# Expert steps and half of a feed-forward layer put in a hand-given order, with weight conversions cut into three parts

## The chip, the core and the metric

The kernel runs on one core of a Trainium2 chip. The core has a matrix engine (PE, TensorE; PEld is its weight load), a vector engine (DVE), a scalar engine (ACT), GpSimd (POOL) and a queue engine (SP) that issues most of the transfers. Each engine works through its own list of instructions in order and waits at an instruction until what it needs is there. The metric is the device time of one execution in microseconds.

## The reference

Three layers follow one another. Linear attention gives x, 2304 tokens by 512. A mixture of 8 experts sends each token to the expert of its largest gate value; an expert is a 512 x 1024 matrix, a ReLU and a 1024 x 512 matrix, and the result is scaled by the gate. The second layer is dense:

```
h = np.maximum(np.einsum('ecd,edf->ecf', disp, w1), 0.0)
y = np.einsum('ecf,efd->ecd', h, w2)
...
h = x @ w_in
g = np.where(h > 0.0, h, alpha * (np.exp(np.minimum(h, 0.0)) - 1.0))
return (g @ w_out).astype(np.float32)
```

w_in (512 x 2048) and w_out (2048 x 512) come in 64-bit floating point; all else is 32-bit.

## The kernel before, in words

Every float32 matrix is split in a high and a low word (names ending in h and l), and a product is three matmuls: high by high, high by low, low by high (`three`, L588 to L590; L877 to L879 in the last product). The high word is a copy on ACT (L480), the low word a subtraction (L483) on the engine that the caller names.

The attention part sorts the tokens by expert, writes rows to a table in DRAM and leaves in `ids` which row goes where. Then come 64 **expert steps**, eight for each of the experts 0 to 7 (r); u numbers them from 0 to 63 and fc is u's place within its expert. An expert works on a window of columns of the sorted tokens, WIN = 352, 336, 320, 304, 288, 288, 272 and 256 wide. Step u (`step`) loads the weights of step u + 3, does h(u) (12 matmuls into `ph`; then hh on ACT, L607, and hl on DVE, L608), then y(u - 1) (12 matmuls into four `acc`), and splits the weights of step u + 2. In y the third matmul of each triple needs hl.

During expert 0 the 18 tiles of sorted tokens are brought in: a gather on POOL's queue (L494, three buffers, so the gather of tile a + 3 waits for the turn of tile a), a scaling on DVE (L500), and a turn of four transposes on PE (L507) with a copy on ACT (L508) into xT. QUOTA says how many tiles a step turns, and in step 6 (fc == 6) what is left is turned and the next expert's window xh, xl is cut out of xT in one piece (L582, L583). After step 36 a branch (L729) skips a part for overfull experts.

The **second layer** works in four quarters of its hidden units (NQ; four weight units in each) over six blocks of 384 tokens: 96 steps of 12 matmuls into `ph` (`ffn_h`) and 9 into `acc` (`ffn_out`, two steps later), with e on ACT, g on DVE, gh on ACT and gl on DVE between. The first time a block is split into yh (ACT) and yl (POOL) and stored; in later quarters it is loaded.

The 64-bit weights of the second layer are **converted** by integer arithmetic, in 32 halves (w_in and w_out of 16 units): `magnitude` on ACT (L655), five DVE operations in `convert` (L663 to L667), then `split`, with the low word on POOL. `cvt_a` and `cvt_b` have one buffer each. The first quarter's eight halves are converted during the expert steps from u = 28 on, one every third step.

What sets the order: the attention part and the first eight expert steps lie in `tc.manual_schedule()`, where each engine's list follows the program text. From step 8 on (BY_HAND) a scheduler sets the order on each engine, and it may put an operation of a later step ahead of one of an earlier step.

Of the kernel before, what the change touches and what calls it, by code (L numbers as in the profile page):

```python
# [9 lines left out]
F32 = mybir.dt.float32  # L10
# [31 lines left out]
def block_kernel(ctx, tc, qT, k, v, g_norm, w_gate, w1, w2, w_in, w_out, out, cap, **_):  # L42
# [62 lines left out]
    with ExitStack() as actx:  # L105
# [154 lines left out]
        def step(c, n=1):  # L260
            for _ in range(n):
                next(c)
# [312 lines left out]
    def window(r, pieces=1):  # L575
        W = WIN[r]
        xh = xw.tile([P, NP, WIN[0]], F32R, name="xh")
        xl = xw.tile([P, NP, WIN[0]], F32R, name="xl")
        src = xT[:, :, bass.ds(offs[r], W)]
        n = NP // pieces  # L580
        for j in range(0, NP, n):
            nc.scalar.activation(xh[:, j:j + n, :W], src[:, j:j + n], AF.Copy)  # L582
            nc.vector.tensor_tensor(out=xl[:, j:j + n, :W], in0=src[:, j:j + n], in1=xh[:, j:j + n, :W].bitcast(F32), op=ALU.subtract)  # L583
        xwin[r] = (xh, xl)
# [51 lines left out]
    class Prep:  # L636
# [14 lines left out]
        def magnitude(self):  # L651
            if wide:
                self.A = wst.tile([P, C], I32, name="cvt_a", bufs=1)
                self.lo, self.hi = (self.st.rearrange("p (c w) -> p w c", w=2)[:, n] for n in range(2))
                nc.scalar.activation(self.A.bitcast(F32), self.hi.bitcast(F32), AF.Abs)  # L655

        def convert(self):
            if wide:

                A, lo, hi = self.A, self.lo, self.hi  # L660
                Bt = wst.tile([P, C], I32, name="cvt_b", bufs=1)
                f = wst.tile([P, C], I32, name="f", tag="a", bufs=AB)
# [3 lines left out]
                nc.vector.tensor_tensor(out=A, in0=A, in1=Bt, op=ALU.bitwise_xor)  # L666
                nc.vector.scalar_tensor_tensor(out=f, in0=lo, scalar=29, in1=A, op0=ALU.logical_shift_right, op1=ALU.bitwise_or)  # L667
# [10 lines left out]
    pstate = {"n": 0}  # L678

    def prep_early(go):  # L680

        n = pstate["n"]
        if not go or n >= len(preps) + 2:
            return
        if n < len(preps):
            preps[n].load()
        if 1 <= n <= len(preps):
            preps[n - 1].magnitude()

    def prep_late(go):  # L690
        n = pstate["n"]
        if not go or n >= len(preps) + 2:
            return
        if n >= 2:
            preps[n - 2].split()
        if 1 <= n <= len(preps):
            preps[n - 1].convert()
        pstate["n"] = n + 1
# [4 lines left out]
    def second_pass(r, o, t):  # L703
# [9 lines left out]
        for fc in range(NF):  # L713
            a1, a2 = t["a"][fc % 2]
# [10 lines left out]
    def beyond_windows():  # L725
# [3 lines left out]
        with tc.If(nc.values_load(over[0:1, 0:1], engines=mybir.ALL_ENGINES, min_val=-N, max_val=N) > 0):  # L729
# [3 lines left out]
                     a=[[wst.tile([P, C], F32, name=n, tag="a", bufs=AB) for n in ("a1", "a2")] for _ in range(2)])  # L733
# [46 lines left out]
    FIRST = NU - 36  # L780
    BY_HAND = 8

    QUOTA = (1, 2, 2, 3, 2, 2, 3, 0)
    ON_DVE = ()

    def step(u):
# [4 lines left out]
        go = u >= FIRST and (u - FIRST) % 3 == 0 and pstate["n"] < 2 * NC2 + 2  # L791
        expert_load(u + 3)
        prep_early(go)
# [9 lines left out]
        if fc == 6 and r + 1 < E:  # L803
            place(need[r + 1], 0)
        place_ahead(2)
        expert_split(u + 2, nc.vector if u < NF and u in ON_DVE else nc.gpsimd)
        prep_late(go)
        if fc == 6 and r + 1 < E:
            window(r + 1)
        if u == 4 * NF + 4:  # L810
            place(NT, 0)
            beyond_windows()
            mark.clear()
        if u == NU - 2 and cap >= BT:
            y_block_into(0, 4)

    with tc.manual_schedule():
# [14 lines left out]
    while pstate["n"] < 2 * NC2 + 2:  # L832
        prep_early(True)
        prep_late(True)
# [59 lines left out]
    per = NB * NC2  # L894
    for s in range(len(steps) + 2):

        go = s % per in (2, 5, 8, 11, 14, 17, 22, 23)
        prep_early(go)
        if s < len(steps):
            ffn_h(*steps[s])  # L900
# [8 lines left out]
        prep_late(go)  # L909
# [35 lines left out]
```

## Time and profile before

| what | value |
|---|---|
| median of three runs | 741.57 us (740.71 to 860.1) |
| profiled execution | 740.88 us, span 739.1 us |
| granted TensorE clock, mean over the span | 0.98 |
| PE, DVE, ACT, POOL busy | 700.4, 409.3, 349.2, 221.8 us |
| expert steps | about 78.8 to 321.2 us of the span |
| second layer | about 321.2 to 732.9 us of the span |

A busy time of PE includes stretches at the lower clock, so a stretch in which PE is always busy may still be slow. The matmuls overlap: each is shown longer than the distance from one start to the next, and that distance is what a step costs.

### The profile page before, as it was taken

To read this page: it belongs to the slowest core of one execution; us is meant where nothing else is said; L and a number is where in the kernel's file an instruction comes from. 1 tells how busy PE (TensorE), PEld (TensorE's weight loads), DVE (VectorE), ACT (ScalarE), POOL (GpSimd) and SP (SyncE) were. 2 spreads that over 40 slices of the span, in tenths; PEclk is the share of its full clock that TensorE was granted. 3 is DMA by queue.
4 is the path that set the end of the run, shared out by engine and by line. 5 is a ranking of instruction groups with operands and counts; after the bars stand their busy time and mean duration, and the time that the engine had idled before them with its cause. 6 is when DMAs were issued, how large, how long until landed. Compare 5 with 4: busy or idle time off the path is not lost.

```text
span 739.1 us, 11701 instructions
## 1 busy us (share of the span) xinstructions
PE 700.4 (95%) x4310; PEld 649.4 (88%) x4310; DVE 409.3 (55%) x696; ACT 349.2 (47%) x682; POOL 221.8 (30%) x194
## 2 busy tenths in 40 slices
PE   8997888999997999969999989999999999999996
PEld 7986887999997999858999979999899998999985
DVE  4568556843657767697732796334943333333343
ACT  1452556654544656555655654333633334333331
POOL 7221575633434545662222330000400001011112
PEclk9998899999999999998999999999999999999999
DMA  8995767754535766655422464322322222343312
GB/s 286 394 299 139 235 198 251 225 146 153 174 105 175 220 193 188 223 171 194 166 86 86 146 225 151 124 96 86 114 86 86 86 86 95 123 157 139 129 43 85
DMA packets 55425, 117.55 MB, mean 159 GB/s; under 512 B 8000, under 2 KB 21824, under 8 KB 55360
## 3 DMA queue, kind: packets, MB, share of 16 engines
q1 hardware_dynamic: 51744, 107.12, 43.7%
q0 software_dynamic: 2880, 9.59, 3.9%
q8 instruction: 36, 0.59, 0.3%
q14 instruction: 29, 0.24, 0.1%
q10 hardware_dynamic: 736, 0.02, 0.1%
HBM read 97.68 MB, written 19.02 MB: 158 GB/s over the span
## 4 chain that ended last, share of the span: by engine, by line
PE 42%; issue 8%; DVE 5%; POOL 1%; ACT 1%; POOLq 0%; DVEq 0%
PE acc L879 7%; PE acc L878 7%; PE ph L588 7%; PE ph L590 7%; PE ph L589 7%; PE acc L877 7%; POOL out L888 1%; DVE cvt_a L666 1%; DVE f L667 1%; DVE cvt_b L663 1%; ACT cvt_a L655 1%; DVE cvt_a L664 0%; DVE cvt_a L665 0%; DVE gl L483 0%; DVE g L858 0%
## 5 line engine op out<-in xcount | busy, mean ns | idle before, releaser
L590 PE MATMUL ph<-yl,w1h 128*128 128x384 f32 x384 | 129.8, 338 | 0.0
L588 PE MATMUL ph<-yh,w1h 128*128 128x384 f32 x384 | 129.7, 338 | 0.0
L589 PE MATMUL ph<-yh,w1l 128*128 128x384 f32 x384 | 129.3, 337 | 0.0
L858 DVE SCALAR_TENSOR_TENSOR g<-e,ph 128x384 f32<-128x384 f32 x96 | 52.9, 551 | 134.2 <-ACT e L856 134.2
L877 PE MATMUL acc<-w2h,gh 128*128 128x512 f32 x288 | 112.7, 391 | 5.0 <-ACT part L883 2.5
L879 PE MATMUL acc<-w2h,gl 128*128 128x512 f32 x288 | 114.8, 399 | 1.8 <-DVE gl L483 1.8
L483 POOL TENSOR_TENSOR w1l<-a,w1h 128x512 fp32r<-128x512 f32 x62 | 88.1, 1424 | 93.1 <-ACT w1h L480 90.6
L878 PE MATMUL acc<-w2l,gh 128*128 128x512 f32 x288 | 114.2, 396 | 0.0
L855 ACT ACTIVATE e<-ph 128x384 f32<-128x384 f32 x96 | 46.9, 489 | 133.5 <-PE ph L590 133.5
L590 PE MATMUL acc<-hl,w2h 128*128 128x288 f32 (+6 forms) x256 | 78.4, 306 | 6.6 <-DVE hl L608 6.3
L590 PE MATMUL ph<-xl,w1h 128*128 128x288 f32 (+6 forms) x256 | 78.7, 308 | 2.7 <-DVE xl L583 2.7
L480 ACT ACTIVATE gh<-g 128x384 fp32r<-128x384 f32 x96 | 50.3, 524 | 65.3 <-DVE g L858 65.1
L483 POOL TENSOR_TENSOR w1l<-f,w1h 128x512 fp32r<-128x512 f32 x16 | 23.5, 1466 | 190.0 <-ACT w1h L480 190.0
L589 PE MATMUL ph<-xh,w1l 128*128 128x288 f32 (+6 forms) x256 | 78.4, 306 | 1.8 <-PEq L729 1.8
L588 PE MATMUL ph<-xh,w1h 128*128 128x288 f32 (+6 forms) x256 | 79.2, 309 | 0.7 <-ACT xh L563 0.7
L588 PE MATMUL acc<-hh,w2h 128*128 128x288 f32 (+6 forms) x256 | 77.9, 304 | 0.9 <-ACT hh L607 0.9
L589 PE MATMUL acc<-hh,w2l 128*128 128x288 f32 (+6 forms) x256 | 77.3, 302 | 0.0
L483 DVE TENSOR_TENSOR gl<-g,gh 128x384 fp32r<-128x384 f32 x96 | 55.8, 581 | 38.5 <-ACT gh L480 38.5
L588 PEld LDWEIGHTS ph<-yh,w1h 128*128 128x128 f32 x384 | 72.6, 189 | 4.2
L589 PEld LDWEIGHTS ph<-yh,w1l 128*128 128x128 f32 x384 | 72.4, 188 | 4.1
L590 PEld LDWEIGHTS ph<-yl,w1h 128*128 128x128 f32 x384 | 72.3, 188 | 0.0
L483 DVE TENSOR_TENSOR w2l<-a,w2h 128x512 fp32r<-128x512 f32 x64 | 54.8, 861 | 29.1 <-ACT w2h L480 29.1
(157 smaller groups left out, 1265.6 us busy)
## 6 DMA issues: line engine op xcount, KB each, us to landing
a<-w SPq DMA_DIRECT2D x128, 256.0 KB
yh<-y_dram SPq DMA_DIRECT2D x18, 768.0 KB
yl<-y_dram SPq DMA_DIRECT2D x18, 768.0 KB
w<-w_in SPq DMA_DIRECT2D x16, 512.0 KB
w<-w_out SPq DMA_DIRECT2D x16, 512.0 KB
kt<-k SPq DMA_DIRECT2D x18, 256.0 KB
vt<-v SPq DMA_DIRECT2D x18, 256.0 KB
x_dram<-oz_all SPq DMA_DIRECT2D x18, 256.0 KB
```

The source lines that it names most:

```text
L480: return nc.scalar.activation(dst[0], src, AF.Copy)
L483: return engine.tensor_tensor(out=dst[1], in0=src, in1=dst[0].bitcast(F32), op=ALU.subtract)
L588: nc.tensor.matmul(out, lhsT=ah, rhs=bh, start=start, stop=False)
L589: nc.tensor.matmul(out, lhsT=al, rhs=bh, start=False, stop=False)
L590: nc.tensor.matmul(out, lhsT=ah, rhs=bl, start=False, stop=stop)
L655: nc.scalar.activation(self.A.bitcast(F32), self.hi.bitcast(F32), AF.Abs)
L663: nc.vector.tensor_scalar(out=Bt, in0=hi, scalar1=-0x80000000, scalar2=0x40000000, op0=ALU.bitwise_and, op1=ALU.bitwise_xor)
L855: nc.scalar.activation(e, ph[:, :BT], AF.Relu, scale=-1.0)
L858: nc.vector.scalar_tensor_tensor(out=g, in0=e, scalar=-1.0, in1=ph[:, :BT], op0=ALU.add, op1=ALU.max)
L877: nc.tensor.matmul(acc, lhsT=gh[:, ts], rhs=w2h, start=(c == 0), stop=False)
L878: nc.tensor.matmul(acc, lhsT=gh[:, ts], rhs=w2l, start=False, stop=False)
L879: nc.tensor.matmul(acc, lhsT=gl[:, ts], rhs=w2h, start=False, stop=(c == NC2 - 1))
```

## The change

Steps 8 to 64 and the first 48 of the 96 steps of the second layer go into `manual_schedule()` too, so that the program text is the order on each engine; the last 48 stay with the scheduler. A conversion becomes three parts: ACT's magnitude with three DVE operations (part 0), two DVE operations (part 1), and the split. `prep_parts` hands them out one at a time: in the expert steps from u = 9 on at fc = 1, 2, 3 and 7 until the 24 of the first quarter are done, then one in each step of the second layer. The low words of the second layer's weights, and of the experts' weights from the split in step 8 on, are made on DVE. In expert 0 the last tiles are turned in step 5 (fc == 5), and each window is cut out in two halves, at fc 5 and 6. In the second layer gh and gl of the step before come ahead of the new `ffn_h` in the text.

```diff
-    def window(r, pieces=1):
+    def window(r, j0, j1):
+
         W = WIN[r]
...
+        if r not in xwin:
+            xwin[r] = (xw.tile([P, NP, WIN[0]], F32R, name="xh"), xw.tile([P, NP, WIN[0]], F32R, name="xl"))
+        xh, xl = xwin[r]
+        src = xT[:, j0:j1, bass.ds(offs[r], W)]
+        nc.scalar.activation(xh[:, j0:j1, :W], src, AF.Copy)
+        nc.vector.tensor_tensor(out=xl[:, j0:j1, :W], in0=src, in1=xh[:, j0:j1, :W].bitcast(F32), op=ALU.subtract)
...
+        def convert(self, part):
...
+            if part == 0:
...
+                nc.scalar.activation(A.bitcast(F32), hi.bitcast(F32), AF.Abs)
                 nc.vector.tensor_scalar(out=Bt, in0=hi, scalar1=-0x80000000, scalar2=0x40000000, op0=ALU.bitwise_and, op1=ALU.bitwise_xor)
...
+                self.A, self.B, self.lo = A, Bt, lo
+            else:
...
+                nc.vector.tensor_tensor(out=self.A, in0=self.A, in1=self.B, op=ALU.bitwise_xor)
+                nc.vector.scalar_tensor_tensor(out=f, in0=self.lo, scalar=29, in1=self.A, op0=ALU.logical_shift_right, op1=ALU.bitwise_or)
...
-            split_lo(t, self.f, nc.gpsimd)
+            split_lo(t, self.f, nc.vector)
...
+    def prep_parts():
+
+        R = 2 * NC2
+        for q in range(NQ):
+            for n in range(q * R, (q + 1) * R):
+                late = q and n >= (q + 1) * R - 2
+                prep_load(n + 2)
+                preps[n].convert(0)
+                yield
+                preps[n].convert(1)
+                yield
+                if not late:
+                    preps[n].split()
+                    yield
...
-    FIRST = NU - 36
-    BY_HAND = 8
+    APART = 4 * NF + 4
+    FIRST = NF + 1
...
-        if fc == 6 and r + 1 < E:
+        if fc == 5 and r + 1 < E:
             place(need[r + 1], 0)
         place_ahead(2)
-        expert_split(u + 2, nc.vector if u < NF and u in ON_DVE else nc.gpsimd)
-        prep_late(go)
-        if fc == 6 and r + 1 < E:
-            window(r + 1)
-        if u == 4 * NF + 4:
+        expert_split(u + 2, nc.gpsimd if u < NF else nc.vector)
+        if fc in (5, 6) and r + 1 < E:
+            m = NP // 2
+            window(r + 1, (fc - 5) * m, (fc - 4) * m)
+        if FIRST <= u < NU and fc in (1, 2, 3, 7) and done["n"] < 6 * NC2:
+            next(parts)
+            done["n"] += 1
...
-        for u in range(BY_HAND):
+        for u in range(APART + 1):
             mark.clear()
             step(u)
-    for u in range(BY_HAND, NU + 1):
-        step(u)
...
+    with tc.manual_schedule():
+        for u in range(APART + 1, NU + 1):
+            mark.clear()
+            step(u)
...
+    def ffn_step(s):
         if 1 <= s <= len(steps):
             ffn_g(*steps[s - 1])
         if s < len(steps):
             n, c = steps[s]
+            ffn_h(n, c)
...
+        next(parts, None)
+
+    hand = 2 * NB * NC2
+    with tc.manual_schedule():
+        for s in range(hand):
+            ffn_step(s)
+    for s in range(hand, len(steps) + 2):
+        ffn_step(s)
```

**PE at step 5 of expert 0.** `pt<-ident,xg` is a turn, four matmuls for each tile; the rows before it end y(4), those after it begin h(6). Before:

```order
L588 MATMUL acc<-hh,w2h 128x352
L589 MATMUL acc<-hh,w2l 128x352
L590 MATMUL acc<-hl,w2h 128x352
L507 MATMUL pt<-ident,xg 128x128 x4
L588 MATMUL ph<-xh,w1h 128x352
```

With the change (the lines of the file are one lower):

```order
L587 MATMUL acc<-hh,w2h 128x352
L588 MATMUL acc<-hh,w2l 128x352
L589 MATMUL acc<-hl,w2h 128x352
L507 MATMUL pt<-ident,xg 128x128 x16
L587 MATMUL ph<-xh,w1h 128x352
```

Before, one tile (14) is turned here and tiles 15, 16 and 17 follow around y(5) in step 6. Now tiles 14 to 17 are turned in a row ahead of h(6).

**DVE in steps 5 to 7**, one piece of the difference. `xg<-xg,used` is the scaling of a tile, `cvt_b` the first operation of a conversion, `xl` the low word of expert 1's window.

```order
-L608 SCALAR_TENSOR_TENSOR hl<-ph,hh 128x352
-L500 SCALAR_TENSOR_TENSOR xg<-xg,used 128x512 x2
+L607 SCALAR_TENSOR_TENSOR hl<-ph,hh 128x352
+L500 SCALAR_TENSOR_TENSOR xg<-xg,used 128x512 x3
 L483 TENSOR_TENSOR w2l<-a_1258,w2h 128x512
-L608 SCALAR_TENSOR_TENSOR hl<-ph,hh 128x352
-L500 SCALAR_TENSOR_TENSOR xg<-xg,used 128x512
-L663 TENSOR_SCALAR cvt_b<-w_2400 128x512
+L583 ISA
+L583 TENSOR_TENSOR xl<-xT,xh 128x2x336
+L607 SCALAR_TENSOR_TENSOR hl<-ph,hh 128x352
 L483 TENSOR_TENSOR w2l<-a_1338,w2h 128x512
```

The first conversion operation no longer stands ahead of xl, the third scaling has moved up by a step, and half of xl comes a step earlier.

**DVE from the last expert step into the second layer.** `yT<-acc` is the end of the experts, `g` and `gl` the second layer's own operations. Before:

```order
L663 TENSOR_SCALAR cvt_b<-w_5863 128x512
L627 ISA
L627 COPY yT<-acc 128x256
L664 TENSOR_SCALAR cvt_a<-cvt_a 128x512
L665 TENSOR_SCALAR cvt_a<-cvt_a 128x512
L666 TENSOR_TENSOR cvt_a<-cvt_a,cvt_b 128x512
L667 SCALAR_TENSOR_TENSOR f<-w_5863,cvt_a 128x512
L663 TENSOR_SCALAR cvt_b<-w_5984 128x512
L664 TENSOR_SCALAR cvt_a<-cvt_a 128x512
L858 SCALAR_TENSOR_TENSOR g<-e,ph 128x384
```

With the change:

```order
L626 COPY yT<-acc 128x256
L867 SCALAR_TENSOR_TENSOR g<-e,ph 128x384
L659 TENSOR_SCALAR cvt_b<-w_4863 128x512
L660 TENSOR_SCALAR cvt_a<-cvt_a 128x512
L661 TENSOR_SCALAR cvt_a<-cvt_a 128x512
L483 TENSOR_TENSOR gl<-g,gh 128x384
```

Before, conversions of several halves stand on DVE ahead of the first g; now the first g follows the experts' last copies directly, and one part stands between g and gl.

## Rows read from the trace of the kernel before

**Rows 1.** Stretches: start:end, busy us (matmul count and so on), PEclk, DMA share, GB/s.

```profile
120.00:140.00 20.00, 17.16 (x99) 16.34 (x98) 19.70 (x21) 12.79 (x25) 15.02 (x9) 0.91 0.71 216
220.00:240.00 20.00, 15.65 (x105) 15.22 (x104) 14.60 (x19) 9.09 (x18) 8.53 (x6) 0.91 0.52 161
300.00:320.00 20.00, 16.29 (x128) 15.24 (x126) 14.99 (x23) 9.03 (x19) 11.32 (x9) 1.00 0.54 182
320.00:340.00 20.00, 15.77 (x73) 14.12 (x74) 17.53 (x26) 10.45 (x24) 9.46 (x8) 0.83 0.57 195
420.00:440.00 20.00, 17.45 (x88) 15.46 (x87) 18.67 (x29) 11.01 (x23) 7.61 (x5) 1.00 0.57 201
```

**Rows 2.** Waits of PE: who waited for whom, us in total, times, longest.

```profile
PE acc L590 <- DVE hl L608: 6.3, 5, 2.6
PE ph L590 <- DVE xl L583: 2.7, 1, 2.7
PE acc L877 <- ACT part L883: 2.5, 1, 2.5
PE ph L589 <- PEq L729: 1.8, 1, 1.8
```

**Rows 3.** Timeline of ACT: start us, us, operation; pairs of steps at two widths.

```profile
217.35 0.41 ACT L607 ACTIVATE hh<-ph 128x288 fp32r<-128x288 f32 x1 [0.97 <-PE ph L590]
220.53 0.41 ACT L607 ACTIVATE hh<-ph 128x288 fp32r<-128x288 f32 x1 [0.97 <-PE ph L590]
...
299.15 0.39 ACT L607 ACTIVATE hh<-ph 128x256 fp32r<-128x256 f32 x1 [0.77 <-PE ph L590]
302.01 0.38 ACT L607 ACTIVATE hh<-ph 128x256 fp32r<-128x256 f32 x1 [0.80 <-PE ph L590]
```

**Rows 4.** Timeline of PE: first of h(7), h(8), second layer; last matmul.

```profile
115.42 0.40 PE L588 MATMUL ph<-xh,w1h 128*128 128x352 f32 x1
...
119.32 0.32 PE L588 MATMUL ph<-xh,w1h 128*128 128x336 f32 x1
...
321.25 0.34 PE L588 MATMUL ph<-yh,w1h 128*128 128x384 f32 x1
...
732.68 0.39 PE L879 MATMUL acc<-w2h,gl 128*128 128x512 f32 x1
```

**Rows 5.** Chain that ended last: two matmuls at one place of steps 54 apart.

```profile
442.42 0.24 PE acc L878
...
668.50 0.24 PE acc L878
```

**Rows 6.** Timeline of DVE about expert 1's window and the gather of tile 16.

```profile
112.48 0.75 DVE L500 SCALAR_TENSOR_TENSOR xg<-xg,used 128x512 f32<-128x512 f32 x1 [2.83 <-DMA xg<-x_dram,ids]
...
119.31 0.43 DVE L663 TENSOR_SCALAR cvt_b<-w 128x512 int32<-128x512 int32 x1 [4.38 <-DMA w<-w_in]
```

**Rows 7.** Timeline of POOL: gathers of tiles 16 and 17, and a split.

```profile
107.56 1.25 POOL L494 DMA_INDIRECT xg<-x_dram,ids  x1
109.79 0.95 POOL L494 DMA_INDIRECT xg<-x_dram,ids  x1 [0.98 <-PE pt L507]
...
314.42 1.29 POOL L483 TENSOR_TENSOR w1l<-f,w1h 128x512 fp32r<-128x512 f32 x1 [3.23 <-ACT w1h L480]
```

**Rows 8.** Timeline of DVE: operations with POOL idle and beside POOL.

```profile
147.44 0.69 DVE L483 TENSOR_TENSOR w2l<-a,w2h 128x512 fp32r<-128x512 f32 x1 [1.51 <-ACT w2h L480]
...
217.79 0.46 DVE L608 SCALAR_TENSOR_TENSOR hl<-ph,hh 128x288 fp32r<-128x288 f32 x1 [0.68 <-ACT hh L607]
...
313.06 0.43 DVE L664 TENSOR_SCALAR cvt_a<-cvt_a 128x512 f32<-128x512 f32 x1
...
314.47 1.78 DVE L666 TENSOR_TENSOR cvt_a<-cvt_a,cvt_b 128x512 int32<-128x512 int32 x1
...
336.09 0.68 DVE L666 TENSOR_TENSOR cvt_a<-cvt_a,cvt_b 128x512 int32<-128x512 int32 x1
```

**Rows 9.** Timeline of ACT, second layer, end of the first quarter.

```profile
436.83 0.66 ACT L655 ACTIVATE cvt_a<-w 128x512 f32<-128x512 f32 x1 [2.37 <-DVE f L667]
```

More of the change, by code (lines that the diff above doesn't have):

```diff
@@ L573, in first_window @@
         placed["s"] = placed["t"] = need[0]
-    def window(r, pieces=1):
+    def window(r, j0, j1):
         W = WIN[r]
[L577 to L584, printed above, removed]
+        if r not in xwin:
[4 more added lines that the diff above has]
+        nc.vector.tensor_tensor(out=xl[:, j0:j1, :W], in0=src, in1=xh[:, j0:j1, :W].bitcast(F32), op=ALU.subtract)
     def three(out, lhs, rhs, start, stop):
@@ L649, in load @@
                 nc.sync.dma_start(out=self.f, in_=src)
[L651 to L660, printed above, removed]
+        def convert(self, part):
+            if not wide:
+                return
+            if part == 0:
+                lo, hi = (self.st.rearrange("p (c w) -> p w c", w=2)[:, n] for n in range(2))
+                A = wst.tile([P, C], I32, name="cvt_a", bufs=1)
                 Bt = wst.tile([P, C], I32, name="cvt_b", bufs=1)
-                f = wst.tile([P, C], I32, name="f", tag="a", bufs=AB)
+                nc.scalar.activation(A.bitcast(F32), hi.bitcast(F32), AF.Abs)
                 nc.vector.tensor_scalar(out=Bt, in0=hi, scalar1=-0x80000000, scalar2=0x40000000, op0=ALU.bitwise_and, op1=ALU.bitwise_xor)
@@ L665, in convert @@
                 nc.vector.tensor_scalar(out=A, in0=A, scalar1=3, scalar2=0x7fffffff, op0=ALU.logical_shift_left, op1=ALU.bitwise_and)
-                nc.vector.tensor_tensor(out=A, in0=A, in1=Bt, op=ALU.bitwise_xor)
-                nc.vector.scalar_tensor_tensor(out=f, in0=lo, scalar=29, in1=A, op0=ALU.logical_shift_right, op1=ALU.bitwise_or)
+                self.A, self.B, self.lo = A, Bt, lo
+            else:
+                f = wst.tile([P, C], I32, name="f", tag="a", bufs=AB)
+                nc.vector.tensor_tensor(out=self.A, in0=self.A, in1=self.B, op=ALU.bitwise_xor)
+                nc.vector.scalar_tensor_tensor(out=f, in0=self.lo, scalar=29, in1=self.A, op0=ALU.logical_shift_right, op1=ALU.bitwise_or)
                 self.f = f.bitcast(F32)
@@ L674, in split, with prep_load @@
             split_hi(t, self.f)
-            split_lo(t, self.f, nc.gpsimd)
+            split_lo(t, self.f, nc.vector)
     preps = [Prep(u, half) for u in range(NF2) for half in range(2)]
[L678 to L698, printed above, removed]
+    loaded = {"n": 0}
+    def prep_load(n):
+        while loaded["n"] < min(n, len(preps)):
+            preps[loaded["n"]].load()
+            loaded["n"] += 1
+    def prep_parts():
[11 more added lines that the diff above has]
+                    yield
+            if q:
+                for n in range((q + 1) * R - 2, (q + 1) * R):
+                    preps[n].split()
+                    yield
+    parts = prep_parts()
     OW = 320
@@ L732, in beyond_windows @@
                      ph=ps_h.tile([P, C], F32, name="ph"), py=ps_h.tile([P, C], F32, name="py", tag="ph"),
-                     a=[[wst.tile([P, C], F32, name=n, tag="a", bufs=AB) for n in ("a1", "a2")] for _ in range(2)])
+                     a=[[wst.tile([P, C], F32, name=n, tag="a", bufs=AB) for n in ("a1", "a2")]])
             for r, o in todo:
@@ L790, in step @@
         more = r + 1 < E and placed["t"] < need[r + 1]
-        go = u >= FIRST and (u - FIRST) % 3 == 0 and pstate["n"] < 2 * NC2 + 2
         expert_load(u + 3)
-        prep_early(go)
+        if u == FIRST - 1:
+            prep_load(2)
         if u < NU:
@@ L826, in block_kernel @@
         place_ahead(2)
-        for u in range(BY_HAND):
+        for u in range(APART + 1):
             mark.clear()
             step(u)
-    for u in range(BY_HAND, NU + 1):
-        step(u)
-    while pstate["n"] < 2 * NC2 + 2:
-        prep_early(True)
-        prep_late(True)
+    with tc.manual_schedule():
+        for u in range(APART + 1, NU + 1):
+            mark.clear()
+            step(u)
+        for _ in range(6 * NC2 - done["n"]):
+            next(parts)
     xctx.close()
@@ L893, in block_kernel @@
     steps = [(n, c) for n in range(NQ * NB) for c in range(NC2)]
[L894 to L900, printed above, removed]
+    def ffn_step(s):
         if 1 <= s <= len(steps):
```

9 lines of the change are left out of this document (4 added, 5 removed).

## The prediction

> **What bounds the kernel now.** I read the stretches first, to see where PE has nothing to do, then the waits of PE, to see for whom, and then the timelines of the engines at those places. In most stretches from step 8 on PE is busy all of the time. Five stretches of 20 us are the exception [rows 1]: PE is busy for 17.16, 15.65, 16.29, 15.77 and 17.45 us, so it idles for 2.8, 4.4, 3.7, 4.2 and 2.6 us, 17.7 us in all. Three of them also show the granted clock below full speed, 0.91, 0.91 and 0.83, which is a part of the time at the lower level of 1.2 GHz after PE had idled; (1 - 0.91) x 20 = 1.8 us twice and 3.4 us make another 7.0 us. The waits of PE name DVE above all (hl 6.3 us, xl 2.7 us), once ACT, and once the branch of L729, whose 1.8 us stay [rows 2].
>
> In those stretches DVE is busy for 14.6 to 19.7 of 20 us, and POOL works beside it [rows 1]. The rows of single operations show what that costs. The exclusive-or of a conversion takes 0.68 us when POOL is idle and 1.78 us when it starts just after a split of POOL of 1.29 us [rows 7, 8]. And the order is bad: the first operation of a conversion stands ahead of xl in DVE's list and keeps DVE waiting for 4.38 us for a transfer, in a step in which PE needs xl next [rows 6]. So what can be gained lies in the order on DVE and ACT, and in the contention, not in the matmuls.
>
> **What could be gained at most.** The whole time from the first matmul of h(8) on is compared with what its steps take when nothing is waited for. A step of width 288 takes 220.53 - 217.35 = 3.18 us, one of width 256 takes 302.01 - 299.15 = 2.86 us [rows 3], so 0.01 us for each column; by that line 336, 320, 304 and 272 take 3.66, 3.50, 3.34 and 3.02 us. Eight steps of each of experts 1 to 7 make 8 x (3.66 + 3.50 + 3.34 + 3.18 + 3.18 + 3.02 + 2.86) = 181.9 us; y(7), half a step of width 352, adds 1.9 us and the branch 1.8 us: 185.6 us. The trace has 321.25 - 119.32 = 201.9 us [rows 4], so 16.3 us are lost there. In the second layer 54 steps take 668.50 - 442.42 = 226.1 us, 4.187 us each [rows 5]; 96 of them are 401.9 us. The trace has, from 321.25 to 732.68 plus one matmul's distance of 0.23 us, 411.7 us [rows 4]: 9.8 us are lost. Together 26.1 us. The idle time without the branch and the clock make 15.9 + 7.0 = 22.9 us of them; the rest is short gaps and restarts.
>
> Is there more to gain inside a step? The rows say no: the 4.187 us hold over 54 steps. By the Trainium skill, page "TensorE: Matmul & The Clock Gate", section "Back-to-back issue gap", an isolated matmul of N columns follows the last one after N/2.4 + 2.5 ns; by that rule a step would be 12 x 162.5 + 9 x 215.8 ns = 3.89 us, the second layer 28 us shorter, and the sum below about 696 us if the change reached that. The trace disagrees with it for these matmuls, and the change issues the same ones.
>
> **Part by part.**
>
> *Hand order in steps 8 to 64.* DVE's list of a step is now hl, w1l, w2l, and at most one part or half a window. With POOL out of the way the short forms of rows 8 apply: 0.46 + 2 x 0.69 = 1.84 us. Part 0 adds 3 x 0.43 = 1.29 us (cvt_b has no short row here; I take that of cvt_a), part 1 adds 0.68 + 0.69 = 1.37 us (the second priced as a split), a split 0.69 us. The heaviest steps are thus at 3.13 and 3.21 us, against 3.18 us of PE at width 288 and 3.02 us at 272. That is level, but only for two steps on end, and hl is not needed before the next h and one y are through, about a step later. Steps without a part have more than 1 us to spare. So I expect the 16.3 us to go, the idle time at 120 to 123 us and at 232 to 235 us with them. What remains on DVE I bound by 0 and by today's 6.3 us of waits for hl [rows 2], and take 3 us, the middle, since the load of the heavy steps is level with PE's.
>
> *Low words on DVE.* 54 splits of experts' weights at 0.69 us leave POOL for DVE, 37 us, and 32 of converted halves, 22 us. They are in the 1.84 us above and, in the second layer, in 1.37 us or less of one part per step of 4.187 us. Beside gl and g of about half a microsecond each that is hidden. Without that cover a split would cost its 0.69 us.
>
> *From experts to second layer, and quarter 1.* All 24 parts are done before step 64, so DVE and ACT are free when the first g is due. The 9.8 us go: the idle 4.2 us and the low clock of 3.4 us at 320 to 340 us, and the 2.6 us at 420 to 440 us. There ACT's list had a conversion's magnitude, waiting 2.37 us for DVE, ahead of the copies out of `acc` that PE needed [rows 9]; in the new text those copies come first. In the 48 scheduled steps I expect nothing new: as before, PE has no gap there.
>
> *Tiles turned in step 5.* This is the one place that gets worse. The gather of tile 17 starts at 109.79 us, after the turn of tile 14, and nothing in the change makes it earlier. The gather of tile 16 started at 107.56 us and was waited for until 112.48 us, 4.9 us [rows 6, 7]. So tile 17 lands at about 114.7 us, is scaled in 0.75 us and turned in some 0.35 us: h(6) starts at about 115.9 us, h(7) one step of width 352 (3.82 us) later, at 119.7 us instead of 115.42 us [rows 4]: 4.3 us lost. SP's weight loads are ahead by two steps and don't suffer. PE idles meanwhile for longer than the 2.8 us that cost 1.8 us of clock at 120 us; bounds are 0, since the 2.6 us at 420 us cost nothing, and 3.4 us [rows 1]. I take 1.8 us. Together 6.1 us, between 3.3 and 8.
>
> **Sum.** Against the profiled execution: 740.88 - 26.1 + 6.1 + 3 = 723.9 us. The median of the runs is 0.7 us above that execution, so I forecast **724.5 us**, 2.3% faster. The forecast's own range: best 740.88 - 26.1 + 3.3 = 718 us, worst 740.88 - 26.1 + 8 + 6.3 = 729 us, or 719 to 730 us on the scale of the median.
>
> **Rivals.**
>
> *The heavy steps pile up* (0.15). If hl falls behind in the 24 steps with a part, PE waits as at 300 to 320 us, where DVE had as much on its list as it could do and PE idled 3.7 of 20 us [rows 1]. 24 steps of 3.2 us at that rate lose 14 us in place of my 3: 735.5 us. For it speaks the level load, and that w1l waits for ACT's w1h, which waits in turn for a transfer; against it, the half step of slack that hl has.
>
> *DVE becomes the bound of the expert stage* (0.06). The same in all 56 steps from step 8 on, some 179 us, loses 33 us: 754 us, slower than before. It decides where a step without a part needs more than PE's 3.0 us on DVE, that is if the three operations took 1.6 times their short forms. Against it: POOL, beside which they were long, has nothing left in that stage but the last three splits of expert 0 and one block of tokens.
>
> *The scheduled half stalls* (0.12). The scheduler still orders two quarters, now with more on DVE. Two stalls as at 420 to 440 us cost 2 x 2.6 us: 729.7 us. Against it: two of its three quarter changes cost nothing before.
>
> *The wait in step 5 is small* (0.12). If tile 17 lands as fast as a transfer without others beside it, and the clock holds, 3 us less are lost: 721.5 us.
>
> **Chances.** My forecast has 0.55. What this kernel's measurement can tell from no change is taken as 2%, 14.8 us, so faster begins below 726.7 us. The forecast's range lies to about four fifths below that (0.45), the last rival wholly (0.12), and some of the others' spread: faster 0.6. Slower by 2%, over 756.4 us, needs most of what the second rival can bring: 0.04. The rest, 0.36, is within 2%. The range for 8 in 10 runs from 718.5 us to 736 us, which takes in the pile-up and leaves out the second rival and the ends.
>
> **What would show it.** Right: stretches of 20 us between 130 and 300 us, and around the change of layers, with PE at 20.00 and the clock at 1.00; w1l on DVE at about 0.7 us; the exclusive-or at 0.7 us everywhere; PE waiting for xg of tile 17 at about 110 to 116 us with a lower clock after it. Wrong: PE's waits for hl still at 6 us or more, or for gl and gh anywhere after 430 us; a DVE that is busy all through experts 1 to 6; or no wait for tile 17 at all.

## The result, and the profile after

| | before | after |
|---|---|---|
| median of the runs | 741.9 us (4 runs) | 723.07 us (721.96 to 725.91, 4 runs) |
| profiled execution | 740.88 us | 721.96 us, span 720.2 us |
| ratio after to before | | 0.9761, 95% interval 0.9733 to 0.979 |

One of the four executions before took 860.1 us and is left out of the ratio. The kernel became 2.4% faster. The forecast was 724.5 us. In the 20-us stretches of the trace after (columns as in [rows 1]), the five that had lost time before, one where DVE is busiest, and the one with the turns of expert 1's last tiles read:

```profile
100.00:120.00 20.00, 14.59 (x82) 13.43 (x81) 9.04 (x12) 9.32 (x16) 9.62 (x9) 0.85 0.48 141
120.00:140.00 20.00, 20.00 (x127) 20.00 (x127) 14.38 (x24) 10.14 (x21) 2.59 (x2) 0.98 0.59 190
220.00:240.00 20.00, 18.27 (x138) 18.07 (x138) 14.05 (x25) 9.91 (x20) 0.00 (x0) 1.00 0.59 181
300.00:320.00 20.00, 20.00 (x147) 19.74 (x146) 10.36 (x19) 11.78 (x27) 5.82 (x6) 1.00 0.22 89
320.00:340.00 20.00, 20.00 (x103) 18.21 (x102) 13.02 (x22) 12.77 (x27) 7.83 (x7) 1.00 0.50 184
420.00:440.00 20.00, 20.00 (x103) 18.21 (x102) 11.68 (x23) 9.05 (x18) 0.00 (x0) 1.00 0.28 106
500.00:520.00 20.00, 20.00 (x103) 18.21 (x102) 19.65 (x38) 10.74 (x21) 0.00 (x0) 1.00 0.43 158
```

PE is full in four of the five, and in the fifth, 220 to 240 us, only the branch is left. The new loss lies in the first row: 14.59 of 20 us at a clock of 0.85. The stretch from 500 us is worth a look too: DVE is busy for 19.65 of 20 us and PE loses nothing: what fills DVE there, beside g, gl and the sums into `part`, is conversions, and PE waits for none of them.

The waits of PE say the same by name. Beside those of [rows 2], the kernel before had two more at the change of layers:

```profile
PE acc L877 <- ACT gh L480: 2.4, 1, 2.4
PE acc L879 <- DVE gl L483: 1.8, 1, 1.8
```

In the trace after all of these are gone, but for the branch (1.7 us, now at L734). What has grown is the wait for xg of the turns at L507, 1.3 us before; that for xT was 1.6 us before as well:

```profile
PE pt L507 <- DVE xg L500: 4.3, 3, 2.5
...
PE pt L507 <- ACT xT L508: 1.6, 2, 0.8
```

The timeline of PE after, with what answers to [rows 4] and, above it, the three turns of tiles 15 to 17, gives the size of each part:

```profile
110.85 0.66 PE L507 MATMUL pt<-ident,xg 128*128 128x128 f32 x4 [0.78 <-ACT xT L508]
114.02 1.08 PE L507 MATMUL pt<-ident,xg 128*128 128x128 f32 x4 [2.52 <-DVE xg L500]
115.89 1.11 PE L507 MATMUL pt<-ident,xg 128*128 128x128 f32 x4 [0.78 <-ACT xT L508]
116.65 0.64 PE L587 MATMUL ph<-xh,w1h 128*128 128x352 f32 x1
...
122.48 0.32 PE L587 MATMUL ph<-xh,w1h 128*128 128x352 f32 x1
...
126.31 0.32 PE L587 MATMUL ph<-xh,w1h 128*128 128x336 f32 x1
...
312.22 0.34 PE L587 MATMUL ph<-yh,w1h 128*128 128x384 f32 x1
...
713.79 0.39 PE L888 MATMUL acc<-w2h,gl 128*128 128x512 f32 x1
```

Expert stage from h(8) on: 312.22 - 126.31 = 185.9 us, where the working gave 185.6 us without any wait. Second layer: 713.79 + 0.23 - 312.22 = 401.8 us, against 401.9 us. So nothing is lost in either. Step 5: h(7) starts 7.06 us later than in [rows 4], and the transfer that it waits for was itself later by half a microsecond (the gather of tile 17 starts at 110.34 us, not at 109.79 us), so about 6.5 us are due to the turns. Three parts make them up. PE is idle for 0.78 + 2.52 + 0.78 = 4.1 us, of which the kernel before had 0.81 us too, so 3.3 us are new. Its row in the trace before:

```profile
115.03 0.63 PE L507 MATMUL pt<-ident,xg 128*128 128x128 f32 x4 [0.81 <-ACT xT L508]
```

h(6) with y(5) takes 5.83 us where 3.83 us are taken one step later, 2.0 us of clock. Most of the rest is turns at the low clock, 1.1 us each instead of 0.6 us.

The timeline of DVE shows the wait's source; DVE waited 2.96 us for the transfer of tile 16, and then for that of tile 17:

```profile
114.52 0.75 DVE L500 SCALAR_TENSOR_TENSOR xg<-xg,used 128x512 f32<-128x512 f32 x1 [0.60 <-DMA xg<-x_dram,ids]
```

And the groups of DVE after, 126 to 312 us (busy us, mean ns | idle before), show the short forms that the sum used, now for all of them:

```profile
L483 DVE TENSOR_TENSOR w1l<-a,w1h 128x512 fp32r<-128x512 f32 x54 | 37.4, 693 | 3.0
...
L666 DVE SCALAR_TENSOR_TENSOR f<-w,cvt_a 128x512 int32<-128x512 int32 x8 | 5.5, 692 | 0.3
L665 DVE TENSOR_TENSOR cvt_a<-cvt_a,cvt_b 128x512 int32<-128x512 int32 x8 | 5.5, 686 | 0.0
...
L659 DVE TENSOR_SCALAR cvt_b<-w 128x512 int32<-128x512 int32 x8 | 3.4, 420 | 0.0
```

The exclusive-or (L665) has a mean of 686 ns, 54 splits of w1l joined DVE at 693 ns each, and the prices taken from neighbours (0.43 us for cvt_b, 0.69 us for f) came out at 0.42 and 0.69 us.

That the total fits doesn't say which part of the change earned it: the order by hand, the low words on DVE, and the three parts came together. The experiments take them apart.

### The profile page after: what moved, and what is told of

The parts are those of the page before. It is cut to its first block, busy times and chain, and to the rows that moved or that the text cites. A ratio compares the mean times of both kernels' runs of the same rounds, so it can differ in the third digit from the quotient of the medians.

```text
span 720.2 us, 11582 instructions
## 1 busy us (share of the span) xinstructions
PE 692.4 (96%) x4310; PEld 645.6 (90%) x4310; DVE 425.3 (59%) x789; ACT 347.8 (48%) x689; POOL 96.9 (13%) x108
## 4 chain that ended last, share of the span: by engine, by line
PE 59%; issue 8%; POOL 1%; POOLq 0%; DVE 0%
PE ph L587 10%; PE ph L589 10%; PE ph L588 10%; PE acc L887 8%; PE acc L888 8%; PE acc L886 8%; PE acc L589 2%; PE acc L587 2%; PE acc L588 2%; POOL out L897 1%; POOLq L952 0%; DVE part L894 0%; POOLq L897 0%
## 5 line engine op out<-in xcount | busy, mean ns | idle before, releaser
L589 PE MATMUL acc<-hl,w2h 128*128 128x288 f32 (+6 forms) x256 | 76.9, 301 | 0.0
L606 ACT ACTIVATE hh<-ph 128x288 fp32r<-128x288 f32 (+6 forms) x64 | 27.1, 423 | 81.0 <-PE ph L589 81.0
L888 PEld LDWEIGHTS acc<-w2h,gl 128*128 128x128 f32 x288 | 54.0, 187 | 11.6
L887 PEld LDWEIGHTS acc<-w2l,gh 128*128 128x128 f32 x288 | 54.0, 187 | 9.2
```

The source lines that it names most:

```text
L589: nc.tensor.matmul(out, lhsT=ah, rhs=bl, start=False, stop=stop)
L606: nc.scalar.activation(hh[:, :W], ph[:, :W], AF.Relu)
L887: nc.tensor.matmul(acc, lhsT=gh[:, ts], rhs=w2l, start=False, stop=False)
L888: nc.tensor.matmul(acc, lhsT=gl[:, ts], rhs=w2h, start=False, stop=(c == NC2 - 1))
```

## The experiments

All times are medians; the ratios are to the kernel before on the same chip. Its medians were 742.16 us beside the first four kernels, 741.34 us beside the next four (from the conversions in one go to the low words alone) and 741.38 us beside the last four.

### The kernel after, again

No edit, to have it beside the next three. 

> The changed kernel once more, as the base for the runs beside it. Every theory expects 723 us, give or take 1.

Measured: 723.06 us (722.34 to 725.34), ratio 0.9733 (0.9674 to 0.9793).

### The last tiles of expert 1 back in step 6

```diff
-        if fc == 5 and r + 1 < E:
+        if fc == (5 if r else 6) and r + 1 < E:
             place(need[r + 1], 0)
...
-            window(r + 1, (fc - 5) * m, (fc - 4) * m)
+            if r:
+                window(r + 1, (fc - 5) * m, (fc - 4) * m)
+            elif fc == 6:
+                window(1, 0, m)
+                window(1, m, NP)
```

> The changed kernel, but in expert 0 the last tiles are turned in step 6 as before, around y(5), and expert 1's window is cut out there in two halves one after the other. All other experts as changed. If the wait for tile 17 in step 5 and the low clock after it cost what I worked out (6.1 us; the trace of the change has h(7) 6.5 us later than the kernel before), the time is 717 us. If the window, now a step later, makes PE wait in its turn at h(8), as it did before, most of that comes back: 720 to 723 us.

Measured: **717.77 us** (716.35 to 718.19), ratio 0.9667 (0.9608 to 0.9726), 5.3 us below the kernel after beside it, as the first of the two expectations said. In its timeline of PE y(5) stands ahead of the turns of tiles 16 and 17, and one wait of 1.07 us is left among them:

```profile
115.91 0.63 PE L507 MATMUL pt<-ident,xg 128*128 128x128 f32 x4 [1.07 <-ACT xT L508]
...
120.20 0.32 PE L587 MATMUL ph<-xh,w1h 128*128 128x336 f32 x1
```

Its h(8) starts at 120.20 us, not at 126.31 us: 6.1 us earlier. Its stretch from 100 to 120 us has the clock at 1.00:

```profile
100.00:120.00 20.00, 17.60 (x117) 16.81 (x116) 10.25 (x15) 11.73 (x22) 11.12 (x10) 1.00 0.56 165
```

Against the same stretch of the kernel after, PE has 3.0 us less idle time and the clock gives back 0.15 x 20 = 3.0 us. The wait in step 5 is thus shown, by size and by place: y(5) is the work that covers the transfer.

### Low words back on GpSimd, order by hand kept

```diff
-            split_lo(t, self.f, nc.vector)
+            split_lo(t, self.f, nc.gpsimd)
...
-        expert_split(u + 2, nc.gpsimd if u < NF else nc.vector)
+        expert_split(u + 2, nc.gpsimd)
```

> The changed kernel, but the low words of w1 of all experts and of the converted weights are made on POOL again, as before the change. The order is still given by hand. Theory 1 (it was the order): 723 to 727 us, since DVE has less to do and longer operations, and PE's waits for hl stay near 0. Theory 2 (it was POOL beside DVE): DVE's operations are long again, PE waits for hl, 733 to 741 us.

Measured: 725.3 us (723.42 to 726.05), ratio 0.9758. As theory 1 said; the contention theory's 733 us and more fell. But the contention itself, DVE held up beside POOL, is there. The groups of DVE, 140 to 300 us:

```profile
L483 DVE TENSOR_TENSOR w2l<-a,w2h 128x512 fp32r<-128x512 f32 x48 | 64.5, 1343 | 23.3 <-ACT w2h L480 21.9 <-PE acc L589 0.6 <-ACTq L734 0.6
L607 DVE SCALAR_TENSOR_TENSOR hl<-ph,hh 128x288 fp32r<-128x288 f32 x16 | 7.3, 454 | 8.7 <-ACT hh L606 8.4
```

Nearly every w2l takes twice its time, 1343 ns on average, and from 126 to 300 us PE waits for nothing but the branch: the long operation falls behind hl, where there is slack. The conversions stay short, the exclusive-or at 678 ns, but not because contention spares them: in this order they stand where POOL is idle. Of their 35 operations from 140 to 300 us one runs beside POOL for more than 0.1 us; in the kernel before it is 19 of 45. A row of POOL and one of DVE from the same step show how:

```profile
244.49 1.29 POOL L483 TENSOR_TENSOR w1l<-a,w1h 128x512 fp32r<-128x512 f32 x1 [0.70 <-ACT w1h L480]
```

```profile
246.25 0.68 DVE L665 TENSOR_TENSOR cvt_a<-cvt_a,cvt_b 128x512 int32<-128x512 int32 x1
```

So in the expert steps contention costs nothing here, where one long operation at most stands ahead of the next hl. It is not shown to be free in the whole kernel: this run is 2.2 us above the kernel after, and PE waits 1.9 us for `part` in the scheduled half, where the kernel after has no wait.

### The scheduler's order back, low words on DVE kept

```diff
-        for u in range(APART + 1):
+        for u in range(NF):
             mark.clear()
             step(u)
-    with tc.manual_schedule():
-        for u in range(APART + 1, NU + 1):
-            mark.clear()
-            step(u)
+    for u in range(NF, NU + 1):
+        step(u)
...
-    hand = 2 * NB * NC2
+    hand = 0
```

> The changed kernel, but from step 8 on and in the whole second layer the scheduler sets the order, as before. Parts, low words on DVE, the turns in step 5 and windows in halves are kept. Theory 1 (order): the losses come back, 735 to 747 us, with waits of PE for hl, xl, gl or gh. Theory 2 (POOL beside DVE): most of the gain stays, 723 to 728 us.

Measured: 725.52 us (721.54 to 728.13), ratio 0.9765. Theory 1, that the order is what counts, fell: without it the time is nearly that of the kernel after. With this and the run before, either the order or the low words' engine could go, and the gain stayed. Two explanations were left: that each of the two is enough, or that the third part, the spread of the conversions, did the work. Four kernels were made to tell these apart.

### Conversions in one go

```diff
                 prep_load(n + 2)
-                preps[n].convert(0)
                 yield
-                preps[n].convert(1)
                 yield
+                preps[n].convert(0)
+                preps[n].convert(1)
                 if not late:
                     preps[n].split()
                     yield
```

> The kernel after, with each half's conversion done in one go: the five operations of the conversion and the split all fall in the third of a half's three calls, the first two calls do nothing. Order by hand and low words on VectorE are kept, nothing is left out. Theory 1 (what frees TensorE is that the conversions are spread thin): such a step now asks VectorE for 1.84 us of steady work, 1.29 + 1.37 + 0.69 us more at once, 5.2 us against some 3.1 us of TensorE; 36 such steps in the expert stage cost 0.1 to 0.25 us each net, so 727 to 732 us. Theory 2 (what frees it is that no instruction stands in front of hl, whether through the order or through the low words' engine): the hh of a step has two steps of slack, so 722 to 725 us.

Measured: 728.58 us (727.71 to 730.29), ratio 0.9821 (0.9777 to 0.9864). 5.5 us above the kernel after, which ran on another chip, and in theory 1's range. That is no support for its sum: it counts 36 steps with a whole conversion in the expert stage, and the edit makes 8, one for each half. No single wait carries it. PE loses 0.1 to 0.4 us in each stretch from 240 to 300 us, and 0.8 us in each of two in the second layer:

```profile
260.00:280.00 20.00, 19.72 (x153) 19.36 (x152) 15.17 (x28) 11.15 (x24) 0.00 (x0) 1.00 0.58 178
280.00:300.00 20.00, 19.62 (x157) 19.21 (x157) 16.09 (x30) 12.09 (x27) 0.00 (x0) 1.00 0.63 196
```

That makes 2.4 us in all. Another 1.8 us of this execution are clock, 0.91 in the stretch of the branch, and the last section shows that such a drop comes in some runs and not in others; so 2.4 us of the difference are shown to belong to the conversions, and the rest is not. The parts help, but without them most of the gain is still there.

### Order by hand alone

The kernel before, with these edits, and with one pair of weight tiles left out in the branch:

```diff
-        for u in range(BY_HAND):
+        for u in range(4 * NF + 5):
             mark.clear()
             step(u)
-    for u in range(BY_HAND, NU + 1):
-        step(u)
+    with tc.manual_schedule():
+        for u in range(4 * NF + 5, NU + 1):
+            mark.clear()
+            step(u)
...
+    hand = 2 * NB * NC2
+    with tc.manual_schedule():
+        for s in range(hand):
+            ffn_step(s)
+    for s in range(hand, len(steps) + 2):
+        ffn_step(s)
```

> The kernel before with one part of the change alone: the expert steps from step 8 on and the first 48 steps of the second layer stand in the order in which they are written. Low words stay on GpSimd, conversions whole and late (from step 28), the last tiles of expert 1 in step 6. (In the branch that is not taken, the pair of weight tiles is one instead of two, for room.) Theory 1 (spreading the conversions did it): 733 to 742 us, since the heavy steps are all there. Theory 2 (order or low words, each enough by itself): the 16.3 + 9.8 us come back without the 6 us in step 5: 715 to 720 us.

Measured: **757.78 us** (756.61 to 761.12), ratio 1.0199 (1.0157 to 1.0242). Both theories fell: the order alone makes the kernel 16 us slower. The order is that of the text before: a conversion stands whole at the end of a step, and gh and gl come behind the new `ffn_h`. The waits of PE from 126 to 300 us:

```profile
PE acc L590 <- DVE hl L608: 10.3, 5, 3.8
PE ph L590 <- DVE xl L583: 5.2, 2, 4.0
```

The longest wait for hl ends at 254.08 us. The timelines of POOL, of DVE, and one row of ACT, just before it:

```profile
247.12 1.74 POOL L483 TENSOR_TENSOR w1l<-f,w1h 128x512 fp32r<-128x512 f32 x1
248.82 1.47 POOL L483 TENSOR_TENSOR w1l<-a,w1h 128x512 fp32r<-128x512 f32 x1
251.04 1.27 POOL L483 TENSOR_TENSOR w1l<-a,w1h 128x512 fp32r<-128x512 f32 x1 [0.75 <-ACT w1h L480]
```

```profile
247.64 1.51 DVE L663 TENSOR_SCALAR cvt_b<-w 128x512 int32<-128x512 int32 x1
249.07 1.51 DVE L664 TENSOR_SCALAR cvt_a<-cvt_a 128x512 f32<-128x512 f32 x1
250.61 0.43 DVE L665 TENSOR_SCALAR cvt_a<-cvt_a 128x512 int32<-128x512 int32 x1
251.08 1.78 DVE L666 TENSOR_TENSOR cvt_a<-cvt_a,cvt_b 128x512 int32<-128x512 int32 x1
252.96 0.69 DVE L667 SCALAR_TENSOR_TENSOR f<-w,cvt_a 128x512 int32<-128x512 int32 x1
253.57 0.45 DVE L608 SCALAR_TENSOR_TENSOR hl<-ph,hh 128x288 fp32r<-128x288 f32 x1
```

```profile
250.04 0.41 ACT L607 ACTIVATE hh<-ph 128x288 fp32r<-128x288 f32 x1 [1.73 <-PE ph L590]
```

hh was ready at 250.45 us, and hl came at 253.57 us, behind a whole conversion of 253.57 - 247.64 = 5.93 us. The five operations take 0.42 + 0.42 + 0.43 + 0.69 + 0.69 = 2.65 us in the kernel after; three of them began while a split of POOL ran. Without the 5.93 - 2.65 = 3.3 us that they lost, the conversion would have ended at 250.3 us, before hh was ready: an estimate from these rows, by which this wait would not have come without the contention. The exclusive-or started 0.04 us after one of 1.27 us and took 1.78 us. The Trainium skill, page "SBUF — State Buffer", section "Who interferes with whom", says that an operation of VectorE with two inputs in SBUF and one of GpSimd that reads SBUF do not share: the one that comes second waits for the first to end. The rows agree: 0.04 us after the split's start, then 1.27 us, then about half a microsecond of its own. `cvt_b` and the first `cvt_a` have a single input and took 1.51 us, so they were held up as well.

An order written out keeps the whole conversion ahead of hl; the scheduler had been free to put something else there. In the kernels run here, hand order was good with small pieces (725.3 us) or without POOL beside it (728.58 us), and bad with neither, though in that run with another text.

### Spread alone

The kernel after with both earlier reversals at once: the scheduler's order, and low words on GpSimd; beside the loops as above, the lines are

```diff
-    hand = 2 * NB * NC2
+    hand = 0
...
-            split_lo(t, self.f, nc.vector)
+            split_lo(t, self.f, nc.gpsimd)
...
-        expert_split(u + 2, nc.gpsimd if u < NF else nc.vector)
+        expert_split(u + 2, nc.gpsimd)
```

> The kernel after with the scheduler's order from step 8 on and in the whole second layer, and the low words of the weights back on GpSimd: what is left of the change is the conversions in three parts from step 9 on, the windows in halves and the last tiles in step 5. Theory 1 (spreading did it): 723 to 728 us, as with either of the two undone alone. Theory 2 (order or low words needed): 735 to 748 us, the time before with the 6 us of step 5 on top or in part hidden.

Measured: 739.97 us (737.89 to 742.4, 10 runs), ratio 0.9977 (0.9955 to 0.9999). Theory 2, that order or low words are needed, has its range met: the spread alone brings no gain that shows. Without the 5 to 6 us of step 5, the spread by itself would be worth about 7 us, an estimate from this run and the one with the late turns.

### Low words on DVE alone

The kernel before, with this edit and no other:

```diff
-            split_lo(t, self.f, nc.gpsimd)
+            split_lo(t, self.f, nc.vector)
...
-        expert_split(u + 2, nc.vector if u < NF and u in ON_DVE else nc.gpsimd)
+        expert_split(u + 2, nc.vector if u >= NF else nc.gpsimd)
```

> The kernel before with one part of the change alone: the low words of the first layer's weights from expert 1 on and of the converted weights are made on VectorE. Order, whole conversions from step 28, and the last tiles in step 6 stay as before. Theory 1 (spreading did it): 735 to 745 us; VectorE has more to do in the heavy steps, 5.2 us against 3.1. Theory 2 (order or low words, each enough by itself): operations beside GpSimd fall from 1.78 to 0.68 us, nothing waits for hl: 715 to 722 us.

Measured: **719.67 us** (718.24 to 721.2), ratio 0.9701 (0.9656 to 0.9745). Theory 1 fell, and of theory 2 the half that speaks of low words stands: two lines give 21.7 us, with conversions whole and a scheduler setting the order. PE's and POOL's lists of instructions are the same as before, but for the low words that left POOL. Those of DVE and ACT are not: the scheduler answered the edit with another order, also at places where time was lost. At the change of layers, two conversion operations, 2.66 us of DVE, stand between the first g (328.95 us) and its gl in the kernel before; here the first g is at 312.99 us, and a low word and the next g stand between:

```profile
332.03 0.54 DVE L483 TENSOR_TENSOR gl<-g,gh 128x384 fp32r<-128x384 f32 x1
```

```profile
314.52 0.55 DVE L483 TENSOR_TENSOR gl<-g,gh 128x384 fp32r<-128x384 f32 x1
```

The first fence is the kernel before, the second this run. So what it gives is the worth of the edit; how much of that is shorter operations and how much the scheduler's other order, it doesn't tell. Its waits of PE from 126 to 300 us are one row:

```profile
PE ph L589 <- PEq L729: 1.9, 1, 1.9
```

Its conversions have the short forms too (groups of DVE, 140 to 300 us); in the kernel before, the same two operations took 1115 and 913 ns on average in that time.

```profile
L666 DVE TENSOR_TENSOR cvt_a<-cvt_a,cvt_b 128x512 int32<-128x512 int32 x11 | 7.6, 688 | 0.1
...
L663 DVE TENSOR_SCALAR cvt_b<-w 128x512 int32<-128x512 int32 x11 | 4.6, 423 | 0.1
```

### Each half of the low words by itself

The kernel before, first with the low words of the experts' first-layer weights on DVE:

```diff
-        expert_split(u + 2, nc.vector if u < NF and u in ON_DVE else nc.gpsimd)
+        expert_split(u + 2, nc.vector if u >= NF else nc.gpsimd)
```

> The kernel before with the low words of the first layer's weights from expert 1 on, and only these, made on VectorE; those of the converted weights stay on GpSimd, everything else as before. Between 215 and 321 us of the run before, GpSimd did 25 of the former and 11 of the latter. Theory A (each operation of GpSimd slows what VectorE does beside it, so the 25 matter most while the conversions run): most of the 21.7 us comes back, 720 to 727 us; the rest is lost in the second layer, where 18 operations of the latter kind stay. Theory B (the low words of the converted weights, a queue of GpSimd behind the conversion, are what holds the buffers): little comes back, 732 to 741 us.

Then, instead of it, with those of the converted weights:

```diff
-            split_lo(t, self.f, nc.gpsimd)
+            split_lo(t, self.f, nc.vector)
```

> The other half of the same edit: only the low words of the converted weights on VectorE, those of the first layer's weights of each expert stay on GpSimd, everything else as before. Theory A (25 operations of GpSimd between 215 and 321 us stay beside the conversions): most of the 16 us of the expert stage stays lost, the second layer is free of GpSimd's low words: 728 to 736 us. Theory B (the queue behind the conversion): 718 to 724 us.

Measured: 731.87 us (729.64 to 734.06), ratio 0.9862 (0.984 to 0.9884), and 728.68 us (727.42 to 729.49), ratio 0.9832 (0.9814 to 0.9851). The first time lies just below theory B's range, the second at the lower end of theory A's, so neither theory holds in both: neither kind of low words has most of the loss. 9.5 and 12.7 us come back, 22.2 us together, about what both give at once (21.7 and 19.3 us in two measurements). In the first kernel PE waits for nothing but the branch from 126 to 300 us and stalls about the change of layers, where POOL still splits converted weights beside the conversions; in the second that stall is smaller, and the early stretch stays bad:

```profile
320.00:340.00 20.00, 17.13 (x71) 14.42 (x71) 16.30 (x29) 11.39 (x25) 6.51 (x6) 0.83 0.59 216
```

```profile
120.00:140.00 20.00, 17.29 (x99) 16.75 (x100) 19.22 (x21) 11.97 (x22) 11.32 (x8) 0.91 0.66 198
...
320.00:340.00 20.00, 18.46 (x93) 16.24 (x92) 17.83 (x32) 12.18 (x26) 5.17 (x5) 1.00 0.67 253
```

The first fence is the kernel with first-layer low words on DVE, the second that with the converted ones.

### The two best, side by side

The kernel with the last tiles back in step 6 and that with the low words alone, unchanged, on one chip.

> The kernel after with the last tiles of expert 1 and both halves of its window in step 6, once more, beside the next run on the same chip. Its first run took 717.8 us. If order by hand and spread conversions add something to the low words on VectorE, it stays below the next kernel by about 2 us: 717 to 719 us.

> The kernel before with both kinds of low words on VectorE and nothing else of the change, once more. Its first run took 719.7 us. If order and spread add something, 719 to 721 us; if they add nothing once the low words are moved, the same as the kernel beside it, 717 to 719 us.

Measured: 718.17 us (716.9 to 718.69), ratio 0.9685 (0.9668 to 0.9701), and 722.1 us (720.05 to 726.24), ratio 0.9744 (0.9719 to 0.9769). The intervals don't meet: once the low words are moved, the rest of the change without the early turns adds about 4 us; the second kernel came out a little above its range. In this run of it, the change of layers still costs PE 2.8 us, and the stretch from 120 us as much:

```profile
120.00:140.00 20.00, 17.22 (x112) 17.03 (x111) 18.31 (x28) 14.01 (x26) 0.90 (x1) 1.00 0.72 223
...
300.00:320.00 20.00, 17.19 (x117) 16.06 (x116) 19.78 (x37) 13.10 (x29) 5.04 (x4) 1.00 0.53 181
```

PE in the kernel with late turns has 20.00 us in both. The wait at 120 us is the one of [rows 6]: the first operation of a conversion stands ahead of xl in DVE's list and waits for its transfer, and PE waits for xl. A row of PE's waits and one of DVE's timeline:

```profile
PE ph L590 <- DVE xl L583: 2.8, 1, 2.8
```

```profile
119.33 0.43 DVE L663 TENSOR_SCALAR cvt_b<-w 128x512 int32<-128x512 int32 x1 [4.84 <-DMA w<-w_in]
```

POOL adds to it, since the next w2l runs beside one of its last splits, 1.77 us instead of 0.68 us. The rest of the wait goes with the order, and moving the low words does not remove it. So the version with everything but the early turns is the best of all those run, 3.2% below before and 0.7% below the kernel after.

## Why the prediction was right

**What could be gained.** The 26.1 us were worked out as the distance of each stage from its steps without waits, and both stages came to that: 185.9 us for 185.6, 401.8 us for 401.9. The repeated step of [rows 3] and [rows 5] was the right measure, since the change issues the same matmuls. For the rule of the Trainium skill, page "TensorE: Matmul & The Clock Gate", section "Back-to-back issue gap", which is given there for an isolated matmul and by which the sum would be about 696 us, the trace after shows nothing: a second-layer step still takes the same 4.19 us with PE busy throughout. One reading was short: the prediction found ACT named once among PE's waits, and the waits for gh and gl at the change of layers, 2.4 and 1.8 us, were not in its rows. Its sum goes by steps and not by names, so it did not suffer.

**The left-over on DVE** was the term that was mis-sized. 3 us were taken, between 0 and 6.3; 0.3 us were left in the expert stage. Steps with a part are level with PE, but only two of them stand next to one another, and hl had its slack. The heavy steps did not pile up.

**The wait in step 5** was right in mechanism and nearly in size: 6.1 us forecast (4.3 of lateness, 1.8 of clock), about 6.5 us measured by the trace and 5.3 us by the medians with and without it. Its two sizes were off in opposite directions: 3.3 us of new idle time, not 4.3 us, and about 3 us of clock, not 1.8 us. That they nearly cancel is luck. The two errors of the sum, -2.7 us on DVE and +0.4 us here, are of opposite sign as well, and 723.9 us for the profiled execution met 721.96 us.

**What the prediction attributed wrongly.** It put the 16.3 us of the expert stage down to the order by hand, with POOL out of the way as a help to it. The runs reverse that. POOL out of the way is enough by itself (719.67 and 722.1 us), the order by itself costs 16 us (757.78 us), and with POOL left beside DVE the order pays only if the conversions are cut up (725.3 us). [rows 8], with 1.78 us against 0.68 us, had pointed at it; [rows 6], with the conversion ahead of xl, is mainly a fault of the order, which came back with POOL out of the way and had the larger part in a wait of 2.8 us there. So the forecast was right on what there was to gain and on the price of step 5, and the whole change came out as forecast because it held the low words too.

**The rivals.** The heavy steps did not pile up, DVE did not become the bound though it was full from 500 to 520 us, and the scheduled half did not stall: from 340 to 700 us PE is busy in every stretch. It did stall, for 1.9 us, in the run with low words on GpSimd. The small wait in step 5 did not come either; tile 17 was scaled 114.52 - 110.34 = 4.2 us after its gather had begun, where 4.9 us were taken, but that gather began 0.55 us later, and its turn waited for xT and ran at the low clock.

**What stays open.** How the 21.7 us of the low words divide between shorter operations and the scheduler's other order on DVE and ACT was not taken apart. The longest wait for hl in the kernel with order alone speaks for the operations, since no scheduler chose there. How the gain splits between order and spread once the low words are moved, some 4 us together, was not taken apart. Why the order alone is as bad as 16 us was traced at its longest wait for hl only, not at each.

## What to carry to other kernels

When a vector operation appears in two durations in one trace, look at what GpSimd was doing in the long ones before changing any order: two lines that moved work from the less busy engine to the busier one gave as much as the whole change here. Where both engines must keep such operations, cut long sequences so that their pieces fit where GpSimd is idle and at most one long operation stands ahead of what the matrix engine needs next. Where a scheduler sets the order, look at the lists again after an edit: moving work changes the order of what was not moved. And when several edits come at once and the sum fits, run each alone before crediting one; here the likeliest-looking one cost time by itself.

## What the runs showed of the hardware

Contention depends on the operation. In the run with low words on GpSimd, w2l, which reads two tiles of weights, took 1343 ns on average beside POOL, while hl at width 288, which reads `ph` and hh, kept 454 ns, as [rows 8] has it with 0.46 us; 9 of those 16 ran in part beside POOL. The same page and section of the Trainium skill says that a VectorE operation with at most one input in SBUF keeps clear of GpSimd, unless it runs in one of the performance modes that use both ports. The pair of groups agrees with it. One input alone is no safeguard: `cvt_b`, with one, took 1.51 us beside POOL in the run with order alone and 0.42 us in the kernel after.

The branch's idle time did not fix the clock after it. In the kernel with the scheduler's order and in that with late turns PE waited 2.1 us for it. The stretch with that wait shows a granted clock of 0.91, so a part of it at 1.2 GHz, in the first (upper row), and 1.00, 2.4 GHz throughout, in the second:

```profile
220.00:240.00 20.00, 17.89 (x124) 17.69 (x123) 11.71 (x20) 9.65 (x18) 0.00 (x0) 0.91 0.48 145
```

```profile
220.00:240.00 20.00, 17.87 (x135) 17.67 (x134) 13.76 (x26) 10.62 (x22) 0.00 (x0) 1.00 0.55 176
```

The difference is 0.09 x 20 = 1.8 us, so two single executions that are 2 us apart may differ in nothing else.
